# Regrouping the retention products of chunks 4 to 7 in a fused RetNet and squared-ReLU FFN kernel

## The chip, the cores and the metric

The kernel runs on one core of a Trainium2 chip. The metric is device time in microseconds of the whole program. Before the change it is 948.77 us, the median of three runs (946.12 to 950.59).

## What is computed

```python
scores = (q @ k.T) / sqrt(64)                      # 8 batches, 8 heads, 576 positions, head size 64
ret    = scores * gamma_h ** (i - j), 0 where j > i
attn   = ret @ v
x      = attn, laid out as 4608 tokens x 512        # heads side by side
h      = maximum(x @ w_in, 0)                       # 512 -> 2048
out    = (h * h) @ w_out                            # 2048 -> 512
```

The weights arrive as 64-bit values, and the kernel rounds them to 32 bits itself, piece by piece, while it runs. "fp32" here is the type of everything that TensorE multiplies.

## The kernel before, in words

**Chunks and blocks.** The 4608 tokens are 36 chunks of 128 tokens. Four chunks make a block of 512, so there are nine blocks. Chunks 0 to 3 are handled by whole-chunk products in a prologue (`scores_full`, `carry_full`, `retain_full`). From chunk 4 on each chunk is two halves of 64 positions. A half needs four kinds of small TensorE products of 64x64: the scores k q (`score`, L468, called line L472 in the trace), "own", the masked scores times v (`own_of`, L599, trace line L601), "carry", the running state times q (L516 in `retain_b`, L636 in `whole`), and "grow", which adds k v of this half to the running state in PSUM tile `u_ps` (`grow_of`, L587, trace line L595). After each grow, `grown` (L495) copies `u_ps` to one of three SBUF tiles `u_sb` on ScalarE, from which a later carry reads. A sequence has nine halves; the state starts anew after the ninth, so the first half of chunk 4 ends a sequence.

**Two ways to order the products.** For chunks 4 to 7 the kernel before splits the work of a chunk in three parts with other TensorE work between them: `retain_a` (L498: own of half 1 and grow of half 0), `retain_b` (L506: carry) followed by `scores` of the next chunk, and `retain_c` (L520: own of half 0 and grow of half 1, then the copy of the result to the FFN's input, `x_out`, L567). From chunk 8 on all of it is one group, `whole(i)` (L616): own and grow, half of the scores of chunk i+1, carry, own and the grow of chunk i+1's first half, and the other half of the scores.

**Transposes.** q and k must lie with the head dimension on the partitions. For chunks up to 8 TensorE does it (`turn`, L448: `turn_in` puts 16 transposes into PSUM, `turn_out` copies the two halves to the SBUF tile `qk`, one on ScalarE and one on VectorE, `engines=(0, 1)`). From chunk 9 on (`N_TURN`) VectorE transposes 32x32 blocks (`flip`, L403, trace line L407) and ScalarE puts them in place with 16 small copies, which are queued in `moves` and issued by `move` (L419, trace line L422) a few at a time. A copy may be issued from two steps after its flip on; `move(C, i)` at the head of iteration i issues all that chunks up to i still lack.

**FFN steps between the groups.** In the steady part seven steps of a later FFN product (`ffn_in`, L727) stand between two groups. Block 0 is different: its 16 steps (`first_in`, L694, matmuls on L704) run while w_in is still being rounded. A step takes one PSUM buffer of the pool `ps_f` (three buffers), a ReLU on ScalarE (L710), and a square. Before a step `convert(6)` issues the six parts of one 64-bit weight piece: VectorE lines L218, L222, L229, L232 and L235, and one ScalarE part (L226) that needs the result of L218. Step j of block 0 needs piece j; the piece issued just ahead of it in the loop is j+2. The prologue issues pieces 0 to 5 and step 0 to step 3; twelve steps are left for the loop over i = 5 to 8, in portions of 2, 3, 3, 3 and 1.

**Queues.** The order on every engine is the order in which the Python code issues (a schedule by hand). One queue, SyncE's, issues nearly all DMAs: `load` (q, k, v of a chunk, L155 and L157; rings of 3, 5 and 4 buffers), `fetch_raw` (64-bit weight pieces, L205; eight buffers) and the stores of h (L716). GpSimd scales q and v in place with the decay factors (`scale_q` L382, trace line L386; `scale_v` L487, trace line L490), in the order of issue.

PSUM has eight banks: three of `ps_f`, two of `ps_x` (results), one of `ps_u` (state), two of `ps_t`, which before the change holds the transposes and the scores in turn.

Of the kernel before, what the change touches and what calls it, by code (L numbers as in the profile page):

```python
# [15 lines left out]
C = 128  # L16
# [24 lines left out]
def kernel(  # L41
# [52 lines left out]
    def pos(i, h):  # L94
        return (2 * i + h) % N_SEQ

    def grows(i, h):
        return i < N_CH and pos(i, h) < N_SEQ - 1
# [81 lines left out]
    def rows(half, n=64):  # L180
        return slice(64 * half, 64 * half + n)
# [208 lines left out]

    N_TURN = 9
    ps_t = [None]
    N_ONE = N_TURN - 1
    moves = []

    def new_qk(i):
# [28 lines left out]
    def turn_in(i, js=(1, 0)):  # L425

        if "p" not in st[i]:
            if i < N_EARLY:
                p = [ps_e.tile([128, 512], F32, tag=f"e{h}", name="t_ps") for h in range(2)]
            else:  # L430
                t = ps_t[0].tile([128, 2, 512], F32, tag="t", name="t_ps")
                p = [t[:, h, :] for h in range(2)]
            st[i]["p"] = [x.rearrange("p (j d t) -> p j d t", j=2, d=HP) for x in p]
        for j in js:
            for hp in range(HP):
                for h in range(2):
                    nc.tensor.transpose(st[i]["p"][h][:, j, hp, :], loaded[i][j][rows(h), 2 * hp:2 * hp + 2, :],  # L437
                                        ident[rows(h), rows(h)])
# [36 lines left out]
    def masked(i):  # L475

        sc, both = st[i]["sc"], st[i]["both"]
        r = st[i]["ret"] = st[i]["kT"].rearrange("p (e a) (b t) -> p e (a b) t", e=2, b=2)
        if i < N_EARLY:
            for e in range(2):  # L480
                nc.vector.tensor_tensor(r[:, e, :, :], sc[e], msk[:, 0, :, :].to_broadcast([C, HP, CH]), op=ALU.mult)
        else:
            nc.vector.tensor_tensor(r, both, msk.to_broadcast([C, 2, HP, CH]), op=ALU.mult)
        if i < N_ONE:
            scale_v(i)

    def scale_v(i):  # L487
        vs = st[i]["vs"] = loaded[i][2]
        at = i % N_PAT
        nc.gpsimd.tensor_tensor(vs, vs, dv[:, :, at:at + 1].to_broadcast([C, H, D]), op=ALU.mult)  # L490
# [3 lines left out]

    def grown(i, h):  # L495
        nc.scalar.copy(u_sb[(2 * i + h + 1) % 3], u_ps[0])  # L496

    def retain_a(i):  # L498

        xp[0] = ps_x.tile([128, 2, 256], F32, tag="x", name="x_ps", padded_shape=[128, 2, 512])  # L500
        clean.clear()
        st[i]["made"] = beside_each(own_of(i, 1, 1), grow_of(i, 0), range(0, H, 2))[-1]
        if grows(i, 0):
            grown(i, 0)

    def retain_b(i):  # L506

        s = st[i]
        if not grows(i, 0):
            wait_for(s["made"])  # L510
        for h in (1, 0):
            if pos(i, h) == 0:
                continue
            u = u_sb[(2 * i + h) % 3]
            for hp, e, b in HEADS[0:2] + HEADS[4:6] + HEADS[2:4] + HEADS[6:8]:
                s["read"] = nc.tensor.matmul(  # L516
                    x_at(hp, e, b, h), lhsT=u[rows(e), hp, :], rhs=s["qT"][rows(e), hp, CH * h:CH * h + CH],
                    start=clears(b, e), stop=False, skip_group_check=True)

    def retain_c(i):  # L520

        own, grow = own_of(i, 0, 0), grow_of(i, 1)
        beside_each(own, grow, (0, 2))
        wait_for(st[i]["read"])
        beside_each(own, grow, (4, 6))
        x_out(i, lambda: grown(i, 1) if grows(i, 1) else None)

    def scores_full(i):

# [37 lines left out]
    def x_out(i, after):  # L567

        n, at = divmod(i * C, TOK)

        while steps and steps[0][0] <= n - 2:
            if i >= N_ONE:
                move(2)
            step()
        if i < N_EARLY:
            after()
        nc.scalar.copy(xT[n][:, :, at:at + C].rearrange("p (g a) t -> p a g t", a=2),
                       xp[0][:, :, 0:256].rearrange("p a (g t) -> p a g t", g=2))
        if i >= N_EARLY:
            after()  # L580
        if at + C == TOK:
            steps.extend(block_steps(n))
            n_next[0] += 1
        st[i] = loaded[i] = None


    def grow_of(i, h):  # L587

        if not grows(i, h):
            return []  # L590
        begins = pos(i, h) == 0
        if begins:
            u_ps[0] = ps_u.tile([128, HP, D], F32, tag="u", name="u_ps")
        u = u_ps[0]
        return [lambda hp=hp, e=e, b=b: nc.tensor.matmul(  # L595
            u[rows(e), hp, :], lhsT=loaded[i][1][rows(h), 2 * hp + e, :], rhs=st[i]["vs"][rows(h), head(hp, e), :],
            start=(begins and hp == 0), stop=(hp == HP - 1), skip_group_check=True) for hp, e, b in HEADS]

    def own_of(i, h, first):  # L599
        s = st[i]  # L600
        return [lambda hp=hp, e=e, b=b: nc.tensor.matmul(  # L601
            x_at(hp, e, b, h), lhsT=s["vs"][rows(h), head(hp, e), :], rhs=s["ret"][rows(h), e, hp, :],
            start=clears(b, e), stop=False, skip_group_check=True)
            for e_ in (first, 1 - first) for hp, e, b in (HEADS[j] for j in (e_, e_ + 4, e_ + 2, e_ + 6))]
# [5 lines left out]
    def beside_each(own, grow, js):  # L610
        made = []
        for j in js:
            made.extend(f() for f in own[j:j + 2] + grow[j:j + 2])
        return made
# [212 lines left out]
                transfers.pop(0)[1]()  # L827

    n_next = [0]
    n_scaled = [N_EARLY + 2]  # L830

    N_0 = N_W1
    done = [0]

    def ffn(i, half):

        if steps and steps[0][0] == 0:

            for _ in range(2 if half and i > N_EARLY else 1):
                if steps and steps[0][0] == 0:
                    move(6)
                    convert(6)
                    for f in flips[:1]:
                        f()
                    del flips[:1]
                    step()
            return
        count = N_MP * NP * C // TOK  # L850
        while steps and count:
            held[0] = count <= 1

            due = sum(m[0] <= i + 2 for m in moves)
            move(max(2, min(4, -(-due // (count - 1)))) if count > 1 else 0)
            ahead[0] = count
            busy[0] = len(flips) > 0
            for f in flips[:1]:
                f()
            del flips[:1]  # L860
            step()
            count -= 1
        held[0] = busy[0] = False
        ahead[0] = N_DF
# [5 lines left out]
            nc.tensor.matmul(t[:, 0:256], lhsT=idle, rhs=idle[:, 0:1].to_broadcast([128, 256]), start=True, stop=True)  # L870

    def loads(i):
        if i < N_TURN - 1:
            load(i + 3)
            return
        if i == N_TURN - 1:
            load(i + 3, "qk")
        if i + 4 < N_CH:
            load(i + 4, "qk")
        if i + 3 < N_CH:  # L880
            load(i + 3, "v")
# [21 lines left out]
    convert(3)  # L903
    turn(2, (0, 0))
    load(4)
    fetch_raw(3)
    load(5)
    first_in(0, (0,), (0, C))
    scores_full(2)
    scale_q(3, nc.gpsimd)  # L910
# [1 line left out]
    turn(3)  # L912
    retain_full(2)
    load(6)
    convert(3)
    scores_full(3)
    scale_q(4, nc.gpsimd)
# [4 lines left out]
    convert(3)  # L922
    retain_full(3)
    first_in(0, (1,), (0, C))
    load(7)
    convert(6)
    step()
    step()
    convert(6)
    turn(4)  # L930
    step()
    convert(3)
    scores(4)
    scale_q(5, nc.gpsimd)
    convert(3)
    step()
    convert(6)
    for i in range(N_EARLY + 1, N_CH + 1):
        if i > N_ONE:
            move(C, i)  # L940
            whole(i - 1)
            if i + 1 < N_CH:
                scale_v(i + 1)
            loads(i)
            if N_TURN <= i + 2 < N_CH:
                flip(i + 2)
            ffn(i - 1, 2)
        else:
            retain_a(i - 1)
            if i < N_TURN:  # L950
                turn(i)
            move(C, i)
            ffn(i - 1, 0)
            retain_b(i - 1)
            if i < N_CH:
                scores(i)
            retain_c(i - 1)
            if i == N_ONE:
                scale_v(i + 1)
                for f in grow_of(i, 0):  # L960
                    f()
                if grows(i, 0):
                    grown(i, 0)
            if N_TURN <= i + 2 < N_CH:
                flip(i + 2)
            ffn(i - 1, 1)
        if i <= N_ONE:
            loads(i)
        if i == N_ONE:
            ffn(i, 0)  # L970
        if i == N_ONE - 1:
            scale_v(i + 1)
        if i > N_EARLY:
            for j in range(n_scaled[0], min(i + (4 if i > N_TURN - 4 else 3), N_CH)):
                n_scaled[0] += 1
                scale_q(j, nc.gpsimd)
    assert n_next[0] == N_BLK
    first.close()

# [255 lines left out]
```

## Time and profile before

| what | value |
|---|---|
| median of three runs | 948.77 us (946.12, 948.77, 950.59) |
| the profiled execution | 946.5 us, its span 944.8 us |
| granted TensorE clock | 0.999 |
| TensorE busy | 935.9 us, 99% of the span |
| VectorE busy | 768.4 us, 81% |
| ScalarE busy | 351.0 us, 37% |
| GpSimd busy | 83.8 us, 9% |
| chain that ended last | 94% TensorE, 3% VectorE, 1% DMA, 1% issue |

The busy share is the time in which an engine had an instruction at work. Matmuls overlap, so a TensorE that is 99% busy may still be slowed between instructions. The chain is followed back from the last instruction to whatever released each step. A row of the timeline gives start, duration, engine, line, operation, output and input, and in brackets the idle time before it and who ended that. The prologue and the stage that the change touches lie in the first 98 us; what follows is seven FFN steps and one group, over and over, and then the second FFN product.

### The profile page before, as it was taken

What the parts mean: (1) busy time and instruction counts of PE and PEld (TensorE: products, weight loads), DVE (VectorE), ACT (ScalarE), POOL (GpSimd) and SP (SyncE); (2) the same over time, 40 slices, a digit from 0 to 9 for tenths busy, and PEclk for the clock granted to TensorE, in tenths of its full rate; (3) what the DMA queues carried; (4) which work ended last, traced back from release to release, by engine and by line L of the source; (5) the groups of instructions that cost most, each with busy time, mean ns of one, the idle gap of its engine ahead of it and who ended that gap; (6) DMA issues with size and microseconds to landing.
All of it is one profiled execution on the core that took longest, in us unless ns stands there. A gap on an engine that the chain in (4) does not pass through costs nothing.

```text
span 944.8 us, 23245 instructions
## 1 busy us (share of the span) xinstructions
PE 935.9 (99%) x9724; PEld 841.8 (89%) x9724; DVE 768.4 (81%) x1423; ACT 351.0 (37%) x827; POOL 83.8 (9%) x82
## 2 busy tenths in 40 slices
PE   8999999999999999999999999999999999999998
PEld 7554888888888888888888899999999999999998
DVE  5988899979897888878846788888888788787876
ACT  3356757676667676676621100000000000000000
POOL 3304021111111111120000000000000000000000
PEclk9999999999999999999999999999999999999999
DMA  9996665685668565863469973543555452525241
GB/s 224 220 315 161 198 184 159 190 281 166 187 201 272 165 192 168 271 189 113 157 233 357 354 284 130 184 169 133 196 178 182 159 207 105 202 101 178 108 162 46
DMA packets 173673, 181.42 MB, mean 192 GB/s; under 512 B 119168, under 2 KB 134400, under 8 KB 166912
## 3 DMA queue, kind: packets, MB, share of 16 engines
q1 hardware_dynamic: 171472, 179.41, 59.8%
q8 instruction: 76, 1.25, 0.5%
q10 hardware_dynamic: 2096, 0.52, 0.3%
q14 instruction: 29, 0.24, 0.1%
HBM read 109.39 MB, written 70.52 MB: 190 GB/s over the span
## 4 chain that ended last, share of the span: by engine, by line
PE 94%; DVE 3%; DMA 1%; issue 1%; SPq 0%; ACT 0%; DVEq 0%
PE o_b L1077 18%; PE h_b L742 17%; PE o_c L1077 12%; PE o_a L1077 12%; PE h_a L742 12%; PE h_c L742 11%; PE h_ps L704 5%; PE x_ps L601 3%; PE sc_ps L472 1%; DMA k_ld<-in_k_dram 1%; PE x_ps L636 1%; PE u_ps L595 1%; PE t_ps L437 0%; SPq L157 0%; PE sc_ps L534 0%
## 5 line engine op out<-in xcount | busy, mean ns | idle before, releaser
L742 PE MATMUL h_b<-room,w 128*128 128x256 f32 x768 | 181.7, 379 | 1.1 <-DVE room L761 1.1
L422 ACT COPY qk<-flip 32x256 f32<-32x256 f32 x432 | 173.8, 402 | 6.7
L742 PEld LDWEIGHTS h_b<-room,w 128*128 128x128 f32 x768 | 145.7, 190 | 21.8 <-DVE room L761 2.1
L1077 PE MATMUL o_b<-w,room 128*128 128x128 f32 x1168 | 144.1, 275 | 0.0
L1077 PEld LDWEIGHTS o_b<-w,room 128*128 128x128 f32 x1168 | 137.2, 192 | 0.0
L742 PE MATMUL h_a<-room,w 128*128 128x256 f32 x512 | 123.9, 385 | 0.0
L1077 PE MATMUL o_c<-w,room 128*128 128x128 f32 x1008 | 123.0, 275 | 0.0
L742 PE MATMUL h_c<-room,w 128*128 128x256 f32 x512 | 121.0, 379 | 0.0
L1077 PEld LDWEIGHTS o_c<-w,room 128*128 128x128 f32 x1008 | 117.7, 192 | 0.0
L1091 ACT COPY r<-o_a 128x128 f32<-128x128 f32 x53 | 14.1, 266 | 271.1 <-PE o_a L1077 235.5
L742 PEld LDWEIGHTS h_c<-room,w 128*128 128x128 f32 x512 | 97.3, 190 | 13.2
L742 PEld LDWEIGHTS h_a<-room,w 128*128 128x128 f32 x512 | 95.0, 190 | 13.7
L1077 PE MATMUL o_a<-w,a 128*128 128x128 f32 x688 | 85.6, 275 | 0.0
L1077 PEld LDWEIGHTS o_a<-w,a 128*128 128x128 f32 x688 | 81.2, 192 | 0.1
L749 DVE SCALAR_TENSOR_TENSOR room<-room 128x512 f32<-128x512 f32 x96 | 67.5, 703 | 3.3
L386 POOL TENSOR_TENSOR q_ld<-q_ld,dv 128x512 f32<-128x512 f32 x34 | 39.6, 1164 | 285.0 <-DMA q_ld<-in_q_dram 256.8
L704 PE MATMUL h_ps<-room,w 128*128 128x512 f32 (+1 forms) x152 | 58.7, 535 | 0.5 <-DVE w L235 0.5
L601 PEld LDWEIGHTS x_ps<-qk,v_ld 64*64 64x64 f32 x1024 | 38.1, 134 | 12.7 <-issue 12.7
L490 POOL TENSOR_TENSOR v_ld<-v_ld,dv 128x512 f32<-128x512 f32 x36 | 42.6, 1185 | 65.0 <-DMA v_ld<-in_v_dram 60.6
L704 PEld LDWEIGHTS h_ps<-room,w 128*128 128x128 f32 x152 | 25.7, 190 | 25.1 <-issue 23.1
L601 PE MATMUL x_ps<-qk,v_ld 64*64 64x64 f32 x1024 | 48.0, 222 | 0.0
L496 ACT COPY u_sb<-u_ps 128x256 f32<-128x256 f32 x60 | 22.5, 375 | 67.9 <-PE u_ps L595 63.0
(113 smaller groups left out, 1300.2 us busy)
## 6 DMA issues: line engine op xcount, KB each, us to landing
g_dram<-room SPq DMA_DIRECT2D x164, 256.0 KB, 3.8
a<-g_dram SPq DMA_DIRECT2D x30, 1024.0 KB, 6.0
room<-g_dram SPq DMA_DIRECT2D x15, 1024.0 KB, 5.9
w_dram<-w SPq DMA_DIRECT2D x28, 448.0 KB, 4.4
w<-w_dram SPq DMA_DIRECT2D x7, 1792.0 KB, 11.4
out_dram<-room SPq DMA_DIRECT2D x17, 512.0 KB, 3.3
q_ld<-in_q_dram SPq DMA_DIRECT2D x64, 128.0 KB, 3.8
w<-in_moe_w_in_dram SPq DMA_DIRECT2D x16, 512.0 KB, 6.6
```

The source lines that it names most:

```text
L386: engine.tensor_tensor(t, t, dv[:, heads, at:at + 1].to_broadcast(list(t.shape)), op=ALU.mult)
L422: nc.scalar.copy(*moves.pop(0)[2:])
L472: nc.tensor.matmul(st[i]["sc"][e][rows(h), hp, :], lhsT=st[i]["kT"][rows(e), hp, t], rhs=st[i]["qT"][rows(e), hp, t], start=True, stop=Tru ...
L490: nc.gpsimd.tensor_tensor(vs, vs, dv[:, :, at:at + 1].to_broadcast([C, H, D]), op=ALU.mult)
L496: nc.scalar.copy(u_sb[(2 * i + h + 1) % 3], u_ps[0])
L595: return [lambda hp=hp, e=e, b=b: nc.tensor.matmul(u[rows(e), hp, :], lhsT=loaded[i][1][rows(h), 2 * hp + e, :], rhs=st[i]["vs"][rows(h), ...
L601: return [lambda hp=hp, e=e, b=b: nc.tensor.matmul(x_at(hp, e, b, h), lhsT=s["vs"][rows(h), head(hp, e), :], rhs=s["ret"][rows(h), e, hp, ...
L704: nc.tensor.matmul(p, lhsT=w[:, c, :], rhs=xT[0][:, c, :].rearrange("p (h t) -> p h t", h=2)[:, lo:hi, at[0]:at[1]], start=(c == 0), stop= ...
L742: nc.tensor.matmul(p[:, mm, :], lhsT=w[:, c, :], rhs=xs[n][right][:, c, :], start=(j in OPENS and mm == 0 and c == 0), stop=(j in CLOSES a ...
L749: nc.vector.scalar_tensor_tensor(t, t, 0.0, t, op0=ALU.max, op1=ALU.mult)
L1077: nc.tensor.matmul(p, lhsT=s["lefts"][left][:, m, :], rhs=w_out[j][:, m, WO_SLOT[right], :], start=(i in OPENS and m == 0), stop=(i in CLO ...
L1091: nc.scalar.copy(r[:, 0, 0:128], p)
```

## The change

Chunks 4 to 7 use `whole` too. The three `retain_*` functions go. A chunk's transposes (`turn(i + 1)`) now stand at the end of the group of chunk i-1, and both copies out of PSUM go to ScalarE (`engines=(0, 0)`). The transposes take two of the three `ps_f` buffers instead of `ps_t`. The three block-0 steps of an iteration stand together after the group. Before each of them at most four `moves` are issued, where it was six. Loads of q and k are issued one chunk earlier, weight pieces 4 to 7 are spread between the loads instead of standing ahead of them, and the scaling of v moves out of `masked` to fixed places.

```diff
-                t = ps_t[0].tile([128, 2, 512], F32, tag="t", name="t_ps")
-                p = [t[:, h, :] for h in range(2)]
+                p = [ps_f.tile([128, 512], F32, tag="f", name="t_ps") for h in range(2)]
...
-    n_scaled = [N_EARLY + 2]
+    n_scaled = [N_EARLY + 3]
...
-    def ffn(i, half):
+    def ffn(i):
         if steps and steps[0][0] == 0:
-            for _ in range(2 if half and i > N_EARLY else 1):
-                if steps and steps[0][0] == 0:
-                    move(6)
-                    convert(6)
-                    for f in flips[:1]:
-                        f()
-                    del flips[:1]
-                    step()
+            for _ in range((N_W1 - N_EARLY) * C // TOK):
+                move(4)
+                convert(6)
+                for f in flips[:1]:
+                    f()
+                del flips[:1]
+                step()
             return
...
     load(4)
-    fetch_raw(3)
-    load(5)
+    load(5, "qk")
+    fetch_raw(1)
+    load(5, "v")
+    fetch_raw(1)
...
     load(6)
+    fetch_raw(1)
...
-    load(7)
     convert(6)
+    scale_v(4)
     step()
     step()
     convert(6)
     turn(4)
+    load(7, "qk")
+    fetch_raw(1)
+    load(7, "v")
+    scale_q(5, nc.gpsimd)
+    scale_v(5)
     step()
     convert(3)
     scores(4)
-    scale_q(5, nc.gpsimd)
+    turn(5, (0, 0))
+    load(8, "qk")
+    scale_q(6, nc.gpsimd)
     convert(3)
     step()
     convert(6)
     for i in range(N_EARLY + 1, N_CH + 1):
-        if i > N_ONE:
-            move(C, i)
-            whole(i - 1)
...
-        else:
-            retain_a(i - 1)
-            if i < N_TURN:
-                turn(i)
-            move(C, i)
-            ffn(i - 1, 0)
-            retain_b(i - 1)
-            if i < N_CH:
-                scores(i)
-            retain_c(i - 1)
...
+        move(C, i)
+        whole(i - 1)
+        if i + 1 < N_TURN:
+            turn(i + 1, (0, 0))
+        if i + 1 < N_CH:
             scale_v(i + 1)
+        loads(i)
+        if N_TURN <= i + 2 < N_CH:
+            flip(i + 2)
+        ffn(i - 1)
+        for j in range(n_scaled[0], min(i + (4 if i > N_TURN - 4 else 3), N_CH)):
+            n_scaled[0] += 1
+            scale_q(j, nc.gpsimd)
```

More of the change, by code (lines that the diff above doesn't have):

```diff
@@ L392 @@
     ps_t = [None]
-    N_ONE = N_TURN - 1
     moves = []
@@ L483, in masked @@
             nc.vector.tensor_tensor(r, both, msk.to_broadcast([C, 2, HP, CH]), op=ALU.mult)
-        if i < N_ONE:
-            scale_v(i)
     def scale_v(i):
@@ L496, in grown @@
         nc.scalar.copy(u_sb[(2 * i + h + 1) % 3], u_ps[0])
[L498 to L526, printed above, removed]
     def scores_full(i):
@@ L571, in x_out @@
         while steps and steps[0][0] <= n - 2:
-            if i >= N_ONE:
-                move(2)
             step()
@@ L872, in loads @@
     def loads(i):
[L873 to L877, printed above, removed]
         if i + 4 < N_CH:
@@ L938 @@
     for i in range(N_EARLY + 1, N_CH + 1):
-        if i > N_ONE:
-            move(C, i)
-            whole(i - 1)
[L942 to L947, printed above, removed]
-        else:
-            retain_a(i - 1)
-            if i < N_TURN:
-                turn(i)
-            move(C, i)
-            ffn(i - 1, 0)
-            retain_b(i - 1)
-            if i < N_CH:
-                scores(i)
-            retain_c(i - 1)
[L958 to L971, printed above, removed]
-            scale_v(i + 1)
[L973 to L976, printed above, removed]
+        move(C, i)
[3 more added lines that the diff above has]
+        if i + 1 < N_CH:
+            scale_v(i + 1)
+        loads(i)
[5 more added lines that the diff above has]
+            scale_q(j, nc.gpsimd)
     assert n_next[0] == N_BLK
```

## The prediction

> **What bounds the kernel now.** I read the chain that ended last first, then the same chain in order of time over the first 300 us, then the timelines of ScalarE, GpSimd and SyncE where the change moves something. The page says that TensorE sets the end:
>
> ```profile
> PE 94%; DVE 3%; DMA 1%; issue 1%; SPq 0%; ACT 0%; DVEq 0%
> ```
>
> So only what shortens or stalls TensorE's own queue counts. The chain in order of time (start, length, what) shows that queue in the stretch of the change:
>
> ```profile
> 31.57 0.65 PE t_ps L437 x16
> 32.22 3.63 PE h_ps L704 x8
> 35.85 0.62 PE sc_ps L472 x32
> 36.47 3.63 PE h_ps L704 x8
> 40.10 0.61 PE x_ps L601 x16
> 40.72 0.64 PE t_ps L437 x16
> 41.36 3.63 PE h_ps L704 x8
> ...
> 85.40 10.50 PE h_ps L704 x24
> 95.90 0.55 PE x_ps L601 x13
> ...
> 97.91 1.92 PE h_a L742 x8
> ...
> 153.21 1.73 PE h_b L742 x8
> 155.79 0.47 PE x_ps L636 x32
> 156.49 0.24 PE sc_ps L472 x13
> 156.96 1.92 PE h_a L742 x8
> ```
>
> A block-0 step standing alone takes 3.63 us; three together take 10.50, or 3.50 each. Every gap between L704 rows is retention work. The chunk-4-to-7 stage runs from chunk 4's transposes at 31.57 to block 1's first product at 97.91: 66.34 us. A steady group lies between the end of an L742 run (153.21 + 1.73 = 154.94) and the next run's start at 156.96: 2.02 us. TensorE idles once in the stage (timeline, idle time in brackets):
>
> ```profile
> 84.72 0.68 PE L595 MATMUL u_ps<-v_ld,k_ld 64*64 64x64 f32 x16 [1.08 <-ACT u_sb L496]
> ```
>
> The ScalarE timeline round the first `whole` group, chunk 8's, shows the moves of chunk 9 finished before the last ReLU of block 0:
>
> ```profile
> 93.60 1.65 ACT L422 COPY qk<-flip 32x256 f32<-32x256 f32 x4
> 95.28 0.63 ACT L712 ACTIVATE room<-room 128x512 f32<-128x512 f32 x1
> 95.93 0.60 ACT L710 ACTIVATE room<-h_ps 128x512 f32<-128x512 f32 x1
> ```
>
> GpSimd shows when q arrives: its scaling starts as q lands (chunk 5 at 37.20, 6 at 40.90, 7 at 44.36).
>
> ```profile
> 37.20 1.55 POOL L386 TENSOR_TENSOR q_ld<-q_ld,dv 128x512 f32<-128x512 f32 x1 [4.92 <-DMA q_ld<-in_q_dram]
> 44.36 1.23 POOL L386 TENSOR_TENSOR q_ld<-q_ld,dv 128x512 f32<-128x512 f32 x1 [2.21 <-DMA q_ld<-in_q_dram]
> ```
>
> **What the Trainium skill says.** "PSUM — Partial Sum Buffer", section "Engine vs sequencer instructions", says that the queues of ScalarE, VectorE and GpSimd are strict FIFO and that matmuls start and complete in program order. The trace agrees: at 82.10 ScalarE starts an L226 after idling 3.02 us for VectorE's L218, and the ReLU behind it (L710, its matmuls over at 82.01) starts only at 83.25. "TensorE: Matmul & The Clock Gate", "Part 4: PE-mode transpose", says that a transpose ends in PSUM and needs a copy after it; here these are L446 copies of 0.59 us on ScalarE, 0.69 on VectorE. "GPSIMD Engine Reference", "1. Specifications", says that GpSimd shares its SBUF interfaces with VectorE; L218 takes 0.42 us alone and 1.28 at 39.94, beside GpSimd's scaling at 40.90.
>
> **The change part by part.**
>
> *Fewer groups, longer runs of steps.* Gaps before, as starts of neighbouring rows: turn(4) 0.65, scores(4) 0.62, then `retain_a` with `turn` 1.26, 1.29, 1.27, 1.27, then carry, scores and `retain_c` 1.50, 1.56, 1.56 and, for chunk 7, 82.01 to 85.40 = 3.39, which holds the 1.08 of idle and the lone grow of 0.68; chunk 8's group 95.90 to 97.91 = 2.01. The sum is 16.38, and the fourteen steps between are 66.34 − 16.38 = 49.96. After: turn(4) 0.65, scores(4) 0.62, turn(5) 0.64; chunk 4's group without one of two carries (0.24, half of the 0.47 row) 1.78; three groups at 2.02; turns 6 to 8 at 0.64; chunk 8's 2.01. That is 13.68. Steps: two alone and four threes, 7.26 + 42.00 = 49.26. Together 62.94: **3.40 us less**, 2.70 in the groups and 0.70 in the steps. All of it is on TensorE's path.
>
> *The moves, six a step cut to four.* Chunk 9's flip is queued in iteration 7; its copies may go from two steps on, which falls at the first step of iteration 8. Three steps at four make 12 of 16. Four are left for `move(C, 9)`, behind the last ReLU of block 0, and chunk 8's group contains scores(9). That ReLU starts as the step ends (95.93 beside 95.90), ends or hands over 0.5 to 0.6 later, the four take 1.65, and a wakening of TensorE by ScalarE took 0.15 (84.57 to 84.72): about 2.35 after the step's end. The scores would start 0.35 after it (own comes first). **Cost 2.0 us**, in TensorE's queue with carry, own and all of block 1 behind it. Bounds: 0 if ScalarE were far ahead, which it can't be since the ReLU waits for the same step; 2.3 if the copies start only when the ReLU has wholly ended and the wakening takes twice as long. I take 2.0.
>
> *A weight part ahead of a state copy.* Before iteration 5, `convert(6)` puts piece 5's L226 (0.72, or 0.62 to the next start) between the ReLU of step 3 and the copy of `u_ps` in chunk 4's group. The copy then ends about 0.6 + 0.62 + 0.38 = 1.6 after the group's start, TensorE resumes at 1.75, and would want its next grow at 1.0 (own and grow 0.45, scores 0.23, carry 0.24). **Cost 0.7 us.** Bounds 0 (L226 early) and 3.0 (it waits for VectorE as at 82.10). The other groups have the ReLU alone ahead of the copy: it hands over at 0.6, when the grow ends (steady: grow done 155.56, copy 155.62 to 156.00, next grow 156.1), so 0 to 0.2, and I take 0.
>
> *Transposes in `ps_f`.* Each turn takes the buffers of three allocations earlier. Step 2 gets that of step 1, whose ReLU ends at 32.2 as step 2 starts: 0.1 us. Turns 6 to 8 get buffers two or three steps old and the step behind them one whose ReLU has 2.6 us: nothing. The second copy moves from VectorE to ScalarE: it frees VectorE of 0.69 four times and of one idle 2.67 (L446 at 65.59), and adds 0.59 on ScalarE, 8.2 busy us a period of 13.2; hidden, at worst 0.6 a turn where the next group's scores came at once, but 10.5 us of steps lie between.
>
> *Loads, SyncE and GpSimd.* Transfers land in order, each q or k half 0.6 us after the last, v 1.2, a weight piece 1.5. Chunk 5's q now goes ahead of three pieces: about 32.4 instead of 37.05. Chunk 6's q goes ahead of one piece: 39.1, scaled at 40.4, needed by turn(6) at about 42.5 + 0.7. Chunk 7's q goes behind five pieces: v of chunk 6 at 41.5, five at 1.5 is 49.0, q at 50.4, scaled at 51.7; turn(7) stands at 56. Piece 4 lands at 35.1, where L218 took it at 34.87; pieces 6 and 7 at 43.0 and 44.6, taken at 45.19 and 49.84 before. No cost, with margins of 2 to 4 us; if one is gone, each us late is a us on TensorE. Later loads, `scale_v` and the waits of SyncE for h stores lie 10 us ahead of use.
>
> *Conversion.* A piece takes VectorE 2.95 us (L218 at 49.84 to L235's end at 52.84); three with one mask make 9.5 of 13.2. In-order, VectorE now waits at each group for the mask's scores, about 2.5 us, but a piece is issued two steps (7 us) before use. Hidden.
>
> *After the stage* the program is the same and shifts with block 1's start.
>
> Sum: −3.40 + 2.0 + 0.7 + 0.1 = **−0.6 us**, 945.9 against the profiled execution's 946.5. The median shown is 2.3 above that execution; applied to it, 948.77 − 0.6 = **948.2**.
>
> **Rivals.** *Full gain:* the moves and the copy cost nothing, because ScalarE or the waits are finer than I assume. Then −3.4: 945.4. For it speaks that the trace shows no wait on a move; against, four moves stand behind a ReLU in the queue order. *Slower, by late q:* the queue of transfers. Pieces landed up to 2.4 apart between 54 and 57 us, not 1.5; five at 2.2 put chunk 7's q at 54, and GpSimd's scaling at 55.3. From a landing after 55 on, turn(7) waits, and with it `scores(7)` and all behind. Late by 5 us, it gives 948.2 + 5 = 953.2. Against it: pieces at 48.6 to 54.5 came at 1.5. *Absorbed:* from 117.7 to 138.6 the chain runs mostly on VectorE. If that stretch were held by w_out's arrival (first piece taken at 108.88), an earlier start would be given back: 948.8. Against: VectorE waits for TensorE at 117.69, and its w_out loads are issued behind chunk 8's group and move with it.
>
> **How the numbers follow.** Forecast (−2 to +1 us) 0.50, full gain or more 0.23, absorbed 0.10, slower 0.17. A measurement of this kernel tells about 0.5% (4.7 us) from no change. Faster than 944.0 would need more than the full gain: 0.07. Slower than 953.5 needs the q wait at its worst or several stalls: 0.12. Within: 0.81. The range takes in the full gain and most of the late q with 1.5 us of spread of a median: 944.3 to 952.5.
>
> **What would show it.** Right: L704 in runs of 10.5 us; four L422 copies behind the last L710 and a TensorE idle of about 2 us ended by them; about 0.7 us of idle ended by L496 in chunk 4's group; block 1 starting near 97.3. Wrong: TensorE waiting on `t_ps` or GpSimd at turns 6 or 7; no idle at scores(9); a start of block 1 that doesn't carry through to the end.

## The result, and the profile after

The changed kernel takes 953.64 us, the median of six runs (950.0 to 955.64). The kernel before, six runs beside it, takes 947.55. The ratio is 1.0058 with a 95% interval of 1.0032 to 1.0084: slower, by about 5.5 us. The forecast was 948.2, so the time lies outside the range (944.3 to 952.5) and on the other side of no change. The profiled execution is the slowest of the six, 955.64 us with a span of 953.8.

From the first product of block 1 to the end, both profiled executions take 846.94 us. The whole difference lies ahead of it. TensorE starts chunk 4's transposes at 31.28 us (31.50 before) and block 1 at 106.91 (97.84 before), so the stage of the change grew from 66.3 to 75.6 us. The chain of the changed kernel in order of time (start, length, what) shows where; PE is TensorE, ACT ScalarE, SPq SyncE issuing, DMA a transfer under way, and the line numbers are those of the changed kernel:

```profile
43.93 10.50 PE h_ps L667 x24
...
64.23 0.45 SPq L679
64.77 8.53 DMA g_dram<-room
73.41 0.60 ACT room L673
74.00 0.61 ACT w L226
74.61 0.52 ACT room L675
75.13 0.49 ACT room L673
75.62 0.27 ACT u_sb L491
76.02 0.37 PE u_ps L558 x2
76.71 0.32 PE sc_ps L470 x12
77.57 1.05 PE t_ps L435 x16
78.61 11.77 PE h_ps L667 x24
```

This reads backward from TensorE. Chunk 6's group waited for the copy of the state (L491). The copy stood in ScalarE's queue behind two ReLUs of block 0 (L673), and the first of these waited for a DMA: the store of the first quarter of h (L679), which SyncE issued at 64.23 and 64.77 us and which landed at 73.30. ScalarE's timeline and TensorE's list of waits (us in total, times, longest) say the same from the other end:

```profile
73.41 0.60 ACT L673 ACTIVATE room<-h_ps 128x512 f32<-128x512 f32 x1 [10.80 <-DMA g_dram<-room]
```

```profile
PE u_ps L558 <- ACT u_sb L491: 7.3, 2, 6.9
PE sc_ps L470 <- ACT qk L421: 1.3, 2, 0.8
```

Why should a ReLU wait for a store? Block 0 writes its h in quarters of four steps, into two SBUF buffers in turn. Step 8 opens the third quarter and overwrites the buffer of the first, so it may write only after the store has read that. SyncE's timeline shows why the store was late (start, length):

```profile
55.51 1.00 SPq L205 DMA_DIRECT2D w<-in_moe_w_in_dram  x2
56.62 1.38 SPq L157 DMA_DIRECT2D q_ld<-in_q_dram  x2
58.05 3.73 SPq L157 DMA_DIRECT2D k_ld<-in_k_dram  x2
61.82 1.34 SPq L155 DMA_DIRECT2D v_ld<-in_v_dram  x1
63.26 0.87 SPq L205 DMA_DIRECT2D w<-in_moe_w_in_dram  x1
64.23 0.93 SPq L679 DMA_DIRECT2D g_dram<-room  x2
```

In the two traces the first store moved from the 59th of SyncE's DMAs to the 68th. The nine DMAs that now go ahead of it are chunk 8's and 9's q and k and chunk 8's v, and the first TensorE work that needs any of them, chunk 8's transposes, starts at 77.50. SyncE's waits for other engines don't explain the delay: from 42 us to the store they come to 3.8 us, and before to 5.9. Before, the same store was issued here, and by the profile it was its own matmuls that released the ReLU of step 8:

```profile
51.96 1.81 SPq L716 DMA_DIRECT2D g_dram<-room  x2
```

```profile
63.70 0.60 ACT L710 ACTIVATE room<-h_ps 128x512 f32<-128x512 f32 x1 [1.71 <-PE h_ps L704]
```

The stall had a second price. The stretches 69 to 75.9 us and 75.9 to 91 us of the changed kernel (busy us of TensorE, its weight loads, VectorE, ScalarE and GpSimd; granted TensorE clock, 1.00 being full speed; DMA share; GB/s) show a clock below 1.00 in and after the stall:

```profile
69.00:75.90 6.90, 0.13 (x6) 0.00 (x0) 1.22 (x2) 2.47 (x5) 0.00 (x0) 0.89 0.95 243
75.90:91.00 15.10, 14.98 (x128) 7.98 (x132) 13.17 (x20) 7.21 (x13) 4.86 (x4) 0.83 0.58 173
```

These are means: the trace's clock record has 0.50 from 74.32 to 81.15 us and 1.00 before and after. In that time the rest of chunk 6's group, from the end of the idle time on, took 1.48 us where chunk 7's took 0.85, chunk 8's transposes 1.05 instead of 0.64 and the next three steps 11.77 instead of 10.50: 2.3 us more. This table sets the terms of the forecast against TensorE's timeline, as differences of the starts of neighbouring pieces:

| piece | forecast us | measured us |
|---|---|---|
| chunk 4's group, with the weight part ahead of the state copy | 1.78 + 0.7 | 2.57 |
| chunk 5's group | 2.02 | 2.12 |
| chunk 6's group | 2.02 | 9.88 |
| transposes of chunks 6, 7, 8 | 0.64 each | 0.64, 0.64, 1.05 |
| three steps, four times | 10.50 each | 10.50, 10.50, 11.77, 10.50 |
| chunk 7's group | 2.02 | 2.12 |
| chunk 8's group, with the four late moves | 2.01 + 2.0 | 3.97 |

Three entries are off by more than 0.1 us, and together they are 7.86 + 0.41 + 1.27 = 9.54 us. Of these 6.89 are the idle time and 2.3 the slower clock. The stage had been forecast at 62.94 + 2.8 = 65.7 and took 75.6.

### The profile page after: what moved, and what is told of

It reads as the page before. It is cut to its first block, busy times and chain, and to the rows that moved or that the text cites. A ratio compares the mean times of both kernels' runs of the same rounds, so it can differ in the third digit from the quotient of the medians.

```text
span 953.8 us, 23253 instructions
## 1 busy us (share of the span) xinstructions
PE 937.8 (98%) x9724; PEld 843.9 (88%) x9724; DVE 760.9 (80%) x1419; ACT 353.3 (37%) x831; POOL 80.6 (8%) x82
## 3 DMA queue, kind: packets, MB, share of 16 engines
q8 instruction: 76, 1.25, 0.5%
HBM read 109.39 MB, written 70.52 MB: 189 GB/s over the span
## 4 chain that ended last, share of the span: by engine, by line
PE 94%; DVE 3%; DMA 2%; ACT 1%; issue 0%; SPq 0%; DVEq 0%; ACTq 0%
PE o_b L1019 18%; PE h_b L705 17%; PE o_c L1019 12%; PE o_a L1019 12%; PE h_a L705 12%; PE h_c L705 11%; PE h_ps L667 5%; PE x_ps L564 3%; PE sc_ps L470 2%; PE x_ps L599 1%; PE u_ps L558 1%; DMA g_dram<-room 1%; DMA k_ld<-in_k_dram 1%; DVE w L229 0%; PE t_ps L435 0%
## 5 line engine op out<-in xcount | busy, mean ns | idle before, releaser
L558 PE MATMUL u_ps<-v_ld,k_ld 64*64 64x64 f32 x896 | 43.9, 225 | 7.3 <-ACT u_sb L491 7.3
```

The lines of the kernel that those rows point to most:

```text
L558: return [lambda hp=hp, e=e, b=b: nc.tensor.matmul(u[rows(e), hp, :], lhsT=loaded[i][1][rows(h), 2 * hp + e, :], rhs=st[i]["vs"][rows(h), ...
```

## The experiments

Two theories were open. **Store theory**: the store's place behind early loads, through ScalarE, is the loss; the regrouping itself does what the sum said. **Group theory**: the regrouping, with both copies on ScalarE and the transposes in the three `ps_f` buffers, costs the time, and the store is only what shows. A third, **bandwidth theory**, grants that the store is late but blames the volume of early transfers, so that another wait would come if this one went. Each ratio is against runs of the kernel before on the same chip.

### Loads at their old places

```diff
     def loads(i):
+        if i < N_TURN - 1:
+            load(i + 3)
+            return
+        if i == N_TURN - 1:
+            load(i + 3, "qk")
...
     turn(5, (0, 0))
-    load(8, "qk")
...
-        loads(i)
+        if i >= N_TURN:
+            loads(i)
         if N_TURN <= i + 2 < N_CH:
             flip(i + 2)
         ffn(i - 1)
+        if i < N_TURN:
+            loads(i)
```

> The changed kernel with its loads of q, k and v back at the places of before: chunk 8's q and k not in the prologue, and the loads of iterations 5 to 8 behind the block-0 steps, so that the first h store stands at the 56th place of SyncE's queue again instead of the 67th. Store theory (the ReLU of step 8 waits for that store's landing at 73.3 us, and nothing else of the change costs much): the store lands near 63 us, the 6.9 us of TensorE idle ended by the state copy is gone, the granted clock stays at 1.00, and block 1 starts near 97.4 us; time 946.8 to 947.5, the same as before. Group theory (the regrouping itself, with both copies on ScalarE and the transposes in the three buffers, costs the time): the stall stays and the time is 952 to 954.

Measured: 947.57 us, ratio 0.9991 (0.9978 to 1.0005). The store landed at 65.12, the granted clock was 1.00 from 69 to 91 us, chunk 6's group took 2.12, and block 1 started at 98.23. The store stood at the 59th place again (the expectation's 56th and 67th are the 59th and 68th in the traces). The ReLU of step 8 still waited a little, without TensorE noticing:

```profile
65.23 0.60 ACT L673 ACTIVATE room<-h_ps 128x512 f32<-128x512 f32 x1 [1.89 <-DMA g_dram<-room]
```

The loss is gone with the loads put back and every part of the regrouping kept. That falsifies the group theory. The kernel is level with the one before, as the forecast had said of the whole change.

### A third buffer for h

```diff
+    g_first = g_room + [room[:, 5120:7680].rearrange("p (s m t) -> p s m t", s=5, m=2), g_room[1]]
...
-        t = g_room[mp % 2][:, 2:5:2, mm, :] if e else g_room[mp % 2][:, 0:4:3, mm, :]
+        t = g_first[mp][:, 2:5:2, mm, :] if e else g_first[mp][:, 0:4:3, mm, :]
...
-                g_room[mp % 2][:, a:b, :, :].rearrange("p s m t -> p s (m t)")) for a, b in QUARTERS])
+                g_first[mp][:, a:b, :, :].rearrange("p s m t -> p s (m t)")) for a, b in QUARTERS])
```

> The changed kernel with its loads where they are, but the third quarter of h in block 0 (steps 8 to 11) goes to a buffer of its own in free SBUF, so no ReLU waits for the first store. Store theory: no idle in chunk 6's group, though the store still lands at about 73 us; step 12 still waits for the second store, which may cost up to 1 us; time 946.8 to 948.5. Bandwidth theory (the early loads fill the DMA engines and whatever needs data next comes late): another wait appears in its place and the time stays above 950. Group theory: 952 to 954.

Measured: 947.02 us, ratio 0.998 (0.9969 to 0.999). The loads stayed early and the store stayed late (issued at 62.92, landed at 70.52), yet ScalarE's waits between 55 and 95 us hold no store, and chunk 6's group took 2.12:

```profile
ACT room L674 <- PE h_ps L668: 10.9, 9, 1.7
ACT room L541 <- PE x_ps L565: 3.1, 3, 1.0
ACT w L227 <- DVE w L219: 1.2, 2, 1.0
```

No other wait came in its place, so the bandwidth theory falls too: what hurt was one wait on one late transfer.

### The kernel before with one load moved up

```diff
         if i < N_TURN - 1:
-            load(i + 3)
+            load(i + 3, "v" if i == N_EARLY + 1 else "qkv")
             return
...
             if i < N_TURN:
                 turn(i)
+            if i == N_EARLY + 1:
+                load(i + 3, "qk")
             move(C, i)
```

> The kernel before with one edit: chunk 8's q and k (four DMAs, 0.5 MB) are loaded right behind chunk 5's transposes, ahead of the first h store, not behind it. Store theory: in the kernel before the ReLU of step 8 follows its matmuls at 63.70 us with the store landing at about 63.5, so there is hardly any slack; four more DMAs ahead put the landing at 66 to 70, and the ReLU waits 2 to 6 us, of which TensorE sees 0 to 3 since one more step and a group lie between; time 947.5 to 951. Group theory: nothing changes, 947.5.

Measured: 950.05 us, ratio 1.002 (1.0009 to 1.003), slower. The store landed at 68.71, and the ReLU of step 8 took its turn there:

```profile
68.81 0.60 ACT L710 ACTIVATE room<-h_ps 128x512 f32<-128x512 f32 x1 [5.88 <-DMA g_dram<-room]
```

In the next group TensorE idled 1.44 us for the state copy behind that ReLU and 0.52 for a copy of transposes on VectorE. So the same kind of loss comes without any regrouping, from four DMAs, at about a third of its size (1.002 against 1.0058). The kernel before ran close to it: its ReLU of step 8 started at 63.70 as its matmuls ended, the first half of the store had landed at 62.44, and the last semaphore update of the second half stands at 63.59 in the trace. The slack was about 0.1 us.

### Six moves ahead of a step

This is the first experiment with one more edit.

```diff
-                move(4)
+                move(6)
```

> The first kernel of this series (loads at the places of before) with six instead of four moves issued ahead of a block-0 step. If the four copies behind the last ReLU cost what the trace shows (chunk 8's group took 3.97 us, not 2.01), the group goes back to about 2.0 and the time falls by 2.0 against that kernel, to 944.8 to 945.5. Rival: the six copies ahead of each step delay the ReLUs of steps 13 and 14 so far that the steps wait instead, and nothing is gained.

Measured: 945.65 us, ratio 0.9972 (0.9963 to 0.9982), and against the first experiment 1.9 us less. Chunk 8's group took 2.01 us, with no idle. ScalarE's timeline shows the last moves ahead of the last ReLU again:

```profile
92.14 1.65 ACT L421 COPY qk<-flip 32x256 f32<-32x256 f32 x4
93.82 0.63 ACT L675 ACTIVATE room<-room 128x512 f32<-128x512 f32 x1
94.36 0.58 ACT L673 ACTIVATE room<-h_ps 128x512 f32<-128x512 f32 x1
```

The forecast's term of 2.0 us for four late moves is confirmed in size and place. The rival didn't come: the ReLUs of steps 13 and 14 were later, but the steps didn't wait.

### The weight part ahead of the state copy

Two tries to take away the 0.44 us of idle in chunk 4's group, on top of the six moves. The first puts piece 5's conversion ahead of step 3.

```diff
-    convert(3)
+    convert(9)
     step()
-    convert(6)
```

> The kernel with six moves and late loads, and piece 5 of the weights converted ahead of step 3 instead of behind it, so that its ScalarE part no longer stands between the ReLU of step 3 and the state copy of chunk 4's group. If that place costs what the trace shows (group of 2.57 us, 0.44 of it idle), the group takes about 2.1 and the time falls by 0.4 to 0.5 us, which five rounds can hardly tell; the trace decides. Rival: the part now waits for VectorE ahead of the ReLU and the ReLU of step 3 is late, so the state copy is no earlier.

Measured: 946.16 us, ratio 0.9987 (0.9977 to 0.9996). The rival held. ScalarE waited for VectorE with the ReLU and the state copy behind it, and TensorE idled 1.78 us instead of 0.44:

```profile
41.58 0.72 ACT L226 ACTIVATE w<-w,exp_bias 128x512 uint32<-128x512 uint32 x1 [3.30 <-DVE w L218]
42.21 0.61 ACT L675 ACTIVATE room<-room 128x512 f32<-128x512 f32 x1
42.73 0.58 ACT L673 ACTIVATE room<-h_ps 128x512 f32<-128x512 f32 x1
43.21 0.36 ACT L491 COPY u_sb<-u_ps 128x256 f32<-128x256 f32 x1
```

The second puts it behind the group.

```diff
     step()
-    convert(6)
     for i in range(N_EARLY + 1, N_CH + 1):
         move(C, i)
         whole(i - 1)
+        if i == N_EARLY + 1:
+            convert(6)
```

> The kernel with late loads and six moves, and piece 5 of the weights converted behind chunk 4's group instead of ahead of it, so that only the ReLU of step 3 stands before the state copy on ScalarE. If the place of the weight part costs the 0.44 us of idle seen in that group (2.57 against 2.12 us), the group takes 2.1 and the time falls by 0.4 us, to about 945.2 to 945.8 beside 945.6; a time near this is the best to be had from the change. Rival: the piece comes too late for step 5 and that step waits for VectorE.

Measured: 946.46 us, ratio 0.9974 (0.9962 to 0.9985), not to be told from the six moves alone and above the 945.2 to 945.8 expected. Chunk 4's group took 2.12 with no idle, as expected, but chunk 7's group then idled 1.25 us for the state copy: there ScalarE's L226 had waited 1.79 us for VectorE (at 81.31), with ReLU and copy behind. The gain was spent on the same kind of wait further on. Why VectorE was later there wasn't followed.

### How much of it is the store, once the loads are late

The third buffer once more, on top of the weight part ahead of step 3 (first line of expectation), and alone in the kernel before (second). The edits are those shown.

> The kernel of the run before it, with the third buffer for h as well, so that no early ReLU of block 0 can wait for the first store, whatever the transfers do. Store theory: if the kernels with two buffers meet that wait in some of their executions, the median falls by up to 1 us and the scatter shrinks; time 944.0 to 945.5. Rival: the wait is gone already with the late loads and nothing changes.

> The kernel before, with nothing but the third buffer for h. Store theory: in its profiled execution no ReLU waits for the store, but the slack is near zero, so other executions wait a little; 947.0 to 948.5 with less scatter than the kernel before. The difference between this run and the one above is then the worth of the regrouping without any store in it: 2.5 to 3.4 us expected from the sum of the groups. Group theory: no difference.

Measured: 946.3 us, ratio 0.9987 (0.9978 to 0.9996), and 948.3 us, ratio 1.001 (0.9996 to 1.0024). Neither differs from its kernel without the buffer, nor is the scatter less, and the first lies outside the 944.0 to 945.5 expected. With late loads the store costs nothing, before or after, so the store theory's own guess of a loss of up to 1 us in the kernel before was wrong. The two differ by 2.0 us, below the 2.5 to 3.4 expected; the 1.78 us of idle from the weight part is in the first of them.

### Filler in the stall

```diff
-            both = ps_t[0].tile([128, 2, 512], F32, tag="t", name="sc_ps")[:, :, 0:256].rearrange("p e (h t) -> p e h t", h=HP)
+            full = ps_t[0].tile([128, 2, 512], F32, tag="t", name="sc_ps")
+            st[i]["spare"] = full[:, 0, 256:512]
+            both = full[:, :, 0:256].rearrange("p e (h t) -> p e h t", h=HP)
...
+        if i == 6:
+            for _ in range(10):
+                nc.tensor.matmul(st[i + 1]["spare"], lhsT=ident, rhs=ident[:, 0:1].to_broadcast([128, 256]),
+                                 start=True, stop=True, skip_group_check=True)
         out_of, into = own_of(i, 1, 1), grow_of(i + 1, 0)
```

> The changed kernel as it is, with ten filler matmuls (128x128 by 128x256, into unused columns of the scores' PSUM tile, read by nobody) in chunk 6's group, ahead of the products that wait for the state copy. They keep TensorE busy for 4 to 5 of the 6.9 us that it stood idle there. If the slower clock after the stall (0.83 granted from 75.9 to 91 us) comes from the idle time, the clock stays at 1.00, chunk 8's transposes take 0.64 instead of 1.05 us and the next three steps 10.50 instead of 11.77, and the time falls by about 1.7 us, to 951.5 to 952.5. Rival (the clock drops for another reason, or the filler only lengthens the stage): no gain, 953.5 or more.

Measured: 952.4 us, ratio 1.003 (1.0017 to 1.0043), where the changed kernel has 1.0058 (1.0032 to 1.0084). In the profile ten matmuls that nobody reads kept the clock at 1.00:

```profile
69.00:76.00 7.00, 6.53 (x101) 5.38 (x90) 2.16 (x4) 3.10 (x7) 1.06 (x1) 1.00 1.11 269
76.00:91.00 15.00, 15.00 (x160) 7.72 (x159) 13.75 (x22) 9.12 (x19) 3.64 (x3) 1.00 0.65 186
```

The rest of chunk 6's group took 0.85 us, chunk 8's transposes 0.64 and the steps 10.50. One profile could be chance, but the clocks of all executions agree: 0.995 to 0.997 in each of the six of the changed kernel, 0.998 to 1.000 in all 17 with the filler. By time alone the 2.3 us aren't shown, since the intervals overlap, and in the profile the store also landed 1.5 us earlier (71.76). It still held ScalarE for 9.09 us.

## Why the prediction was wrong, point by point

- **Fewer groups, longer runs (−3.4 us): right in kind, a little smaller.** Four runs of three steps at 10.50 came as forecast; groups took 2.12 where 2.02 was assumed, and chunk 4's, without its idle time, 2.1 where 1.78 was; with these sizes the term is about −2.75. With late loads and six moves the terms of the forecast leave −3.4 + 0.7 + 0.1 = −2.6 us. The stage took 64.6 us against 66.3, so 1.7 less (chunk 4's scores took 0.5 longer in that execution), and the time fell to 0.9972 of before, 2.7 us. Not all of the 2.7 need be the groups: 4 of the 22 executions had a mean clock of 0.998 or less, and 29 of the 67 of the kernel before.
- **Four moves behind the last ReLU (+2.0): right**, 3.97 against 2.01 us, and 1.9 us of time when undone.
- **A weight part ahead of the state copy (+0.7): right in place, uncertain in size**: 0.44 us of idle in the changed kernel and 1.05 in the first experiment. That chunk 4's group came to 2.57 where 1.78 + 0.7 = 2.48 was forecast is luck: this term was 0.26 too large and the group 0.35 too small.
- **Transposes in `ps_f`, copies on ScalarE (+0.1): right.** Chunk 4's transposes took 0.76 us to the next step, where it was 0.65.
- **Loads, SyncE and GpSimd (0): this is the step that failed.** Its last sentence said: "Later loads, `scale_v` and the waits of SyncE for h stores lie 10 us ahead of use." The loads did; the store didn't. I had worked out when each load would land and asked who waits for loads, and not what the loads were put ahead of. In the trace of before, the first store was issued at 51.96, landed at 63.59, and the ReLU that reuses its buffer ran at 63.70: the margin was 0.1 us, not 10. Moved behind nine DMAs of loads that nobody needed yet, the store landed at 73.30. This cost 6.9 us of idle on TensorE, in one group.
- **The clock: not in the sum at all.** 2.3 of the 9.54 us came from the slower clock after the stall.
- **Rivals.** "Slower, by late q" had the right queue and the wrong transfer: chunk 7's q landed at 51.59, near the 50.4 worked out, and turn(7) never waited. That its 953.2 lies near the measured 953.64 is luck. "Absorbed" was wrong: the rest of the program shifted as a block. What the Trainium skill states ("PSUM — Partial Sum Buffer", "Engine vs sequencer instructions"), that ScalarE takes its queue strictly in order, is what carried the loss to TensorE: the state copy had no part in the store, it only stood behind the ReLU. The trace agrees: the ReLU waited 10.80 us, and the copy started at 75.51, after it and three more instructions.
- **Two readings were slightly off, without effect.** Chunk 7's gap of 3.39 us took its two ends from two views; within the timeline it is 3.32. And L218's 1.28 us at 39.94 lie mostly beside GpSimd's scaling of v that began at 39.52, and only at their end beside the one at 40.90.

## What to carry to other kernels

When a change issues loads earlier, list what they are put ahead of in their queue. A store is a release: whoever reuses its buffer waits for it, so its place has a deadline like a load's. Check for each buffer in turns how near the last release was to the next write in the old trace; if it was near zero, everything moved ahead of it can be paid for. And a stall of TensorE can cost more than its own length, through the clock: here 2.3 us on top of 6.9.

## What the runs showed of the hardware that was not expected

Between the first and the last microseconds of the program the clock records of the eleven traces hold only 1.00 and 0.50. Three of them have a stretch at 0.50 there: 6.83 us in the changed kernel, and 3.41 us in the second experiment and in the kernel with the weight part and the third buffer. A mean such as 0.83 is such a stretch averaged with full speed. A stretch of 3.41 us takes 0.0018 off the mean clock of the whole execution, so a listed 0.998 is about one stretch and 0.996 about two (an estimate from these lengths and the spans of about 945 us). Much of the scatter between executions goes with it: in the 67 executions of the kernel before that stand beside the first experiment, the 32 at 1.000 took 947.87 us on average, the 24 at 0.998 949.89 and the 5 at 0.996 951.37.

The clock also fell after idle times far shorter than 6.9 us, but not each time. Two kernels idled 1.76 and 1.78 us in chunk 4's group. In the one with the third buffer the clock was 0.50 from 44.57 to 47.98 us and the three steps took 11.97 us; in the other it stayed at 1.00 and they took 10.50. In the second experiment, chunk 8's group, with 1.31 us of idle, took 5.07 us, the clock being 0.50 from 96.36 on, where the first had taken 3.97 with 1.32 of idle at 1.00. What decides it no run here settles.
